# Two drains in GpSimd's order: a gated linear recurrence with routed experts on one Trainium2 core

## The chip, the cores and the metric

The kernel runs on one core of a Trainium2 chip. The time is that of one execution on the device, in microseconds (us). The engines are TensorE (PE in the profile, with its weight loads as PEld), VectorE (DVE), ScalarE (ACT), GpSimd (POOL) and SyncE (SP). A `q` behind an engine's name, as in POOLq, means its sequencer: instructions such as waits, register moves and drains, which the profile does not count as busy time.

## The reference

A recurrence with complex gates runs over 768 steps for 4 batches of 8 heads of width 48. Its output, 3072 rows of 384, goes through a mixture of 8 experts in which every row is given to one expert:

```python
for t in range(S):
    new_re = ar * S_re - ai * S_im
    new_im = ar * S_im + ai * S_re
    kv = np.einsum('bhd,bhe->bhde', k[:, :, t], v[:, :, t])
    S_re, S_im = (new_re + kv, new_im)
    y[:, :, t] = np.einsum('bhd,bhde->bhe', q[:, :, t], S_re)
...
logits = x @ w_gate                        # x: (3072, 384), 8 experts
expert_idx = np.argmax(logits, axis=1)
...
for e in range(E):                         # the rows of expert e, in sorted order
    h = np.maximum(x_sorted[lo:hi] @ w1[e], 0.0)
    y_sorted[lo:hi] = h @ w2[e]
y = y_sorted[inv_perm]
return (gate_w[:, None] * y).astype(np.float32)
```

## The kernel before

The first half, to about 280 us, computes the recurrence in six chunks of 128 steps and writes the rows `x` to a scratch array `xd` in device memory. While it does so, the router counts which rows go to which expert. The experts are then sorted by the number of their rows into eight **places**. Place 0 is the expert with the most rows; `CAPS = (448, 416, 416, 408, 400, 384, 376, 360)` gives the rows that each place has room for. A place is cut into tiles of 128 rows: four for places 0 to 4, three for places 5 to 7.

The second half is a loop over the places (`for i in range(E)`, L894). For place i:

- `gather` (L574, the instruction at L580) issues one indirect transfer for each tile on GpSimd, which fetches the rows from `xd` into `xg`. The gathers of the next place are written ahead of the expert's work.
- `turn` (L589) transposes the gathered rows on TensorE. The turn of the next place stands between the second-last and the third-last output tile of the present one.
- `expert` (L620) multiplies by the first weights into four buffers `hps`, evicts them with the ReLU on VectorE (L635) and ScalarE (L633) in turn, multiplies by the second weights into `yps`, and scales by the gate into `y` on VectorE (L655, or L666 to L669 for a tile of few rows). `y` comes from a pool `yp` of three buffers.
- `scatter` (L610, the instruction at L611) issues one indirect transfer for each tile on GpSimd, which writes the rows of `y` to their places in the output.
- `load_w` (L563) loads the weights of the place after next, on SyncE's queue.

The two tiles that place 0 does early (`early`, L672) run at the end of the first half. The last output tile of the last place is finished behind a branch: `verdict` (L877) tests whether the input lies in the range that the fast path covers, the branch at L909 leads to a slow path that these inputs do not take, and L1161 and L1162 then scale and scatter the last tile.

A planner of the framework sets the order of the instructions on each engine, from data dependences, priorities in the order of writing, and planned times. So gathers stand further ahead on GpSimd than they are written: those of place 6 are issued while place 3 is finished. `behind` (L70) adds an edge for order alone between two instructions:

```python
def behind(ins, others, reason="order"):
    for o in others:
        tc.add_manual_dep(ins.ins, o.ins.name, NOSYNC, reason=reason)
```

Besides the gathers and scatters, GpSimd issues four small transfers in the first half (L255). At the end of the program the framework puts closing code on every engine (L1186 in the profile): SyncE waits for all semaphores, GpSimd has a drain, and barriers join the engines.

Of the kernel before, what the change touches and what calls it, by code (L numbers as in the profile page):

```python
# [36 lines left out]
def kernel(  # L37
# [12 lines left out]
    nc = tc.nc  # L50
# [13 lines left out]
    T = {}  # L64

    def mm(o, lhsT, rhs, start=True, stop=True):
        T["mm"] = nc.tensor.matmul(o, lhsT=lhsT, rhs=rhs, start=start, stop=stop, skip_group_check=True)  # L67
        return T["mm"]
# [4 lines that stand above are left out]
# [487 lines left out]
    def tiles(i):  # L560
        return -(-CAPS[i] // P)

    def load_w(i, after=None):  # L563
        o = own0 if i == 0 else owner[:, i : i + 1]
        ev = nc.sync.value_load(o[0:1, 0:1], min_val=0, max_val=E - 1)
        wa = EP[i % 2].tile([P, KD, F], FP, tag="wa", name="wa")
        ins = nc.sync.dma_start(out=wa, in_=w1[ds(ev, 1)].rearrange("o (i p) f -> p (o i) f", p=P))
        if after is not None:
            tc.add_manual_dep(ins.ins, after.ins.name, SYNC, reason="rows first")
        wb = EP[i % 2].tile([P, KF, DM], FP, tag="wb", name="wb")  # L570
        nc.sync.dma_start(out=wb, in_=w2[ds(ev, 1)].rearrange("o (i p) d -> p (o i) d", p=P))
        T["w", i] = wa, wb

    def gather(i, t0, t1, rows=N):  # L574

        if t0 == 0:
            T["xg", i] = EP[i % 2].tile([P, CT, DM], FP, tag="xg", name="xg")
        for t in range(t0, t1):
            n = min(P, CAPS[i] - t * P)
            nc.gpsimd.indirect_dma_start(  # L580
                out=T["xg", i][0:n, t],
                out_offset=None,
                in_=xd[0:rows, :],
                in_offset=bass.IndirectOffsetOnAxis(ap=tok[0:n, i, t : t + 1], axis=0),
                bounds_check=rows - 1,
                oob_is_err=False,
            )

    def turn(i, t0, t1, ps, end=None):  # L589

        xg = T["xg", i]
        if t0 == 0:
            T["xt", i] = EP[i % 2].tile([P, KD, CAPS[0]], FP, tag="xt", name="xt")
        c0, c1 = t0 * P, min(CAPS[i], t1 * P)
        for d in range(KD):
            tp = ps.tile([P, 512], FP, tag="tp", name="tp")
            for t in range(t0, t1):
                n = min(P, CAPS[i] - t * P)
                ins = nc.tensor.transpose(
                    out=tp[:, (t - t0) * P : (t - t0) * P + n],  # L600
                    in_=xg[0:n, t, d * P : (d + 1) * P],
                    identity=ident[0:n, 0:n],
                )
                if end is not None:
                    behind(ins, [end])
            T["turned"] = (nc.scalar.copy if d % 2 else nc.vector.tensor_copy)(
                out=T["xt", i][:, d, c0:c1], in_=tp[:, 0 : c1 - c0]
            )

    def scatter(y, n, i, t, to=None):  # L610
        nc.gpsimd.indirect_dma_start(  # L611
            out=out,
            out_offset=bass.IndirectOffsetOnAxis(ap=row[0:n, i, t : t + 1] if to is None else to[0:n], axis=0),
            in_=y[0:n],
            in_offset=None,
            bounds_check=N - 1,
            oob_is_err=False,
        )

    def expert(i, t0, t1, psH, psO, yp, between=None):  # L620

        xt = T["xt", i]
        wa, wb = T["w", i]
        if t0 == 0:
            T["ht", i] = EP[i % 2].tile([P, KF, CAPS[0]], FP, tag="ht", name="ht")
        ht = T["ht", i]
        c0, c1 = t0 * P, min(CAPS[i], t1 * P)
        for f in range(KF):
            ps = psH.tile([P, 512], FP, tag="tp" if psH is psT else "h", name="hps")[:, 0 : c1 - c0]
            for d in range(KD):  # L630
                mm(ps, wa[:, d, f * P : (f + 1) * P], xt[:, d, c0:c1], d == 0, d == KD - 1)
            if f % 2:
                nc.scalar.activation(out=ht[:, f, c0:c1], in_=ps, func=AF.Relu)  # L633
            else:
                ts(out=ht[:, f, c0:c1], in0=ps, scalar1=0.0, scalar2=None, op0=OP.max)  # L635
        for t in range(t0, t1):
            if t == t1 - 2 and between is not None:
                between()
            n = min(P, CAPS[i] - t * P)
            if psO is psA:  # L640
                ps = psO.tile([P, DM], FP, tag="at", padded_shape=[P, 512], name="yps")
            else:
                T["left"] = T.get("left", sum(tiles(j) for j in range(E)) - EARLY) - 1
                po = psO if T["left"] % 2 else EP["last"]
                ps = po.tile([P, DM], FP, tag="y", padded_shape=[P, 512], name="yps")
            g = gate[0:n, i, t : t + 1]
            y = yp.tile([P, DM], FP, tag="y", name="y")
            hs = ht[:, :, t * P : t * P + n]
            if n > 64:
                for f in range(KF):  # L650
                    mm(ps[0:n], hs[:, f], wb[:, f], f == 0, f == KF - 1)
                if i == E - 1 and t == t1 - 1:
                    T["last"] = ps[0:n], g
                    return
                ts(out=y[0:n], in0=ps[0:n], scalar1=g, scalar2=None, op0=OP.mult)  # L655
            else:

                w = 32 if n <= 32 else 64
                parts = P // w
                for f in range(KF):  # L660
                    j = f % parts
                    mm(ps[j * w : j * w + n], hs[:, f], wb[:, f], f < parts, f >= KF - parts)
                z = yp.tile([P, DM], FP, tag="z", name="z")
                for j in range(1, parts):
                    nc.scalar.copy(out=z[j * w : j * w + n], in_=ps[j * w : j * w + n])
                tt(out=y[0:n], in0=ps[0:n], in1=z[w : w + n], op=OP.add)  # L666
                for j in range(2, parts):
                    tt(out=y[0:n], in0=y[0:n], in1=z[j * w : j * w + n], op=OP.add)
                ts(out=y[0:n], in0=y[0:n], scalar1=g, scalar2=None, op0=OP.mult)  # L669
            scatter(y, n, i, t)  # L670

    def early(t0, t1, end):  # L672
# [204 lines left out]
    def verdict():  # L877

        bad = yp.tile([P, NC + 1], FP, tag="bad", name="bad")
        nc.vector.memset(bad, 0.0)  # L880
        ts(out=bad[:, 0:NC], in0=inr, scalar1=float(RW) - 0.5, scalar2=None, op0=OP.is_lt)
        nc.vector.tensor_copy(out=bad[:, NC:], in_=over)
        bp = psG.tile([P, NC + 1], FP, tag="tp", padded_shape=[P, 512], name="bp")
        mm(bp, ones, bad)
        bs = yp.tile([P, 2], FP, tag="bs", name="bs")
        nc.vector.reduce_sum(bs[:, 0:1], bp[:, 0:NC], axis=AX_X)
        nc.vector.reduce_sum(bs[:, 1:2], bp, axis=AX_X)
        nc.vector.tensor_copy(out=flag, in_=bs[0:1])
        ts(out=bs[:, 1:2], in0=bs[:, 1:2], scalar1=0.0, scalar2=float(2 * N), op0=OP.is_gt, op1=OP.mult)
        tt(out=lasts, in0=row[:, E - 1, tiles(E - 1) - 1 : tiles(E - 1)], in1=bs[:, 1:2], op=OP.add)  # L890

    turn(0, EARLY, tiles(0), psG)
    load_w(1, T["turned"])
    for i in range(E):  # L894
        t0 = EARLY if i == 0 else 0
        if i == E - 1:
            verdict()
        if i + 1 < E:
            gather(i + 1, 0, tiles(i + 1))
        expert(i, t0, tiles(i), psH, psO, yp, (lambda: turn(i + 1, 0, tiles(i + 1), psG)) if i + 1 < E else None)  # L900
        if i + 2 < E:
            load_w(i + 2)
        if 1 <= i <= NR_:
            in_range(i - 1)
# [255 lines left out]
    y = ctx.enter_context(tc.tile_pool(name="lasty", bufs=1)).tile([P, DM], FP, name="y")  # L1160
    ts(out=y[0:n], in0=ps, scalar1=g, scalar2=None, op0=OP.mult)  # L1161
    scatter(y, n, E - 1, tiles(E - 1) - 1, lasts)  # L1162


# [26 lines left out]
```

## Time and profile before

| | |
|---|---|
| median of 3 runs | 562.87 us |
| the runs | 561.13 to 563.52 us |
| profiled execution, its own time | 566.46 us |
| span of the profile, first to last instruction | 564.7 us |
| TensorE busy | 533.7 us, 95% |
| GpSimd busy | 68.6 us, 12% |
| last scatter issued | 557.70 us from the span's start |

The span is what the profile covers; the profiled execution's own time is 1.8 us longer. Times within the profile count from the start of the span. A transfer's instruction on GpSimd is busy only while its descriptors are made; the data lands later.

### The profile page before, as it was taken

The page shows a single profiled execution, that of the slowest core. Times are in us where ns is not written, and L with a number is a line of the kernel's source. Part 1 is how long each engine was busy: PE and PEld are TensorE (multiplying, and loading weights), DVE is VectorE, ACT ScalarE, POOL GpSimd, SP SyncE. Part 2 cuts the span into 40 slices and gives each one's busy share as a digit, 9 for nine tenths or more (in the row PEclk, how much of TensorE's full clock was granted, in tenths as well). Part 3 has the DMA queues.
Part 4 walks back from the last instruction along what each step waited for, and adds up shares of the span by engine and source line. Part 5 has one row for each costly group of instructions (what it writes and reads, how often), then busy time and mean ns, then how long its engine had stood idle before and what let it go on. Part 6 is the DMA issues. An engine that isn't in the chain of part 4 may idle for free. (4 is left out here: it accounts for less than half of the span.)

```text
span 564.7 us, 8239 instructions
## 1 busy us (share of the span) xinstructions
PE 533.7 (95%) x3221; PEld 379.9 (67%) x3221; DVE 287.0 (51%) x586; ACT 218.2 (39%) x330; POOL 68.6 (12%) x94
## 2 busy tenths in 40 slices
PE   3889989999999999999899999999999999999994
PEld 2666858877888888888767555555565555565652
DVE  5478688678789889786366264412212131111200
ACT  6867887966678864553200010101101011010000
POOL 2000000000000000001044301503022030100101
PEclk9979979999999999999999999999999999999997
DMA  9976791859655835603549985533235333330000
GB/s 167 187 96 87 126 129 26 160 82 169 114 86 101 151 61 120 98 29 120 190 182 328 387 314 233 183 119 91 102 140 167 113 111 96 127 124 15 26 15 27
DMA packets 166053, 73.39 MB, mean 130 GB/s; under 512 B 147725, under 2 KB 159031, under 8 KB 166008
## 3 DMA queue, kind: packets, MB, share of 16 engines
q1 hardware_dynamic: 162456, 63.12, 48.1%
q0 software_dynamic: 3552, 9.68, 5.0%
q8 instruction: 27, 0.44, 0.4%
q14 instruction: 18, 0.15, 0.1%
HBM read 63.26 MB, written 9.73 MB: 129 GB/s over the span
## 5 line engine op out<-in xcount | busy, mean ns | idle before, releaser
L67 PE MATMUL yps<-wb,ht 128*128 128x384 f32 (+6 forms) x464 | 136.8, 489 | 0.0
L67 PE MATMUL hps<-xt,wa 128*128 128x416 f32 (+7 forms) x432 | 132.5, 465 | 0.0
L67 PEld LDWEIGHTS hps<-xt,wa 128*128 128x128 f32 x432 | 79.9, 190 | 49.8 <-issue 24.1
L67 PEld LDWEIGHTS yps<-wb,ht 128*128 128x128 f32 (+6 forms) x464 | 74.1, 175 | 52.9 <-issue 8.1
L633 ACT ACTIVATE ht<-hps 128x416 f32<-128x416 f32 (+7 forms) x36 | 16.8, 468 | 139.8 <-PE hps L67 128.5
L655 DVE TENSOR_SCALAR y<-yps,gate 128x384 f32<-128x384 f32 (+1 forms) x23 | 14.2, 617 | 99.4 <-PE yps L67 99.3
L67 PE MATMUL at<-qt,kt 96*128 96x128 f32 x384 | 54.2, 281 | 0.5 <-DVE am L334 0.5
L611 POOL DMA_INDIRECT out_dram<-y,row x28 | 28.7, 1023 | 191.4 <-DVE y L655 162.8
L67 PEld LDWEIGHTS at<-qt,kt 96*128 96x128 f32 x384 | 47.6, 191 | 4.8 <-issue 1.9
L635 DVE TENSOR_SCALAR ht<-hps 128x416 f32<-128x416 f32 (+7 forms) x36 | 18.9, 525 | 61.4 <-PE hps L67 61.4
L334 DVE TENSOR_TENSOR am<-at,tri 128x512 f32<-128x512 f32 x48 | 33.0, 688 | 21.0 <-PE at L67 20.9
L67 PE MATMUL yt<-am,v 128*48 128x128 f32 x384 | 43.0, 281 | 0.6 <-DVE am L334 0.6
L580 POOL DMA_INDIRECT xg<-xd,tok x29 | 31.6, 1089 | 78.6 <-PE tp L326 40.4
L67 PE MATMUL yt<-qt,G 96*48 96x128 f32 x320 | 36.7, 274 | 0.0
L326 PE MATMUL tp<-ident,K 128*96 128x128 f32 x192 | 33.7, 288 | 0.7 <-DVE K L317 0.4
L67 PE MATMUL dk<-v,K 128*96 128x48 f32 x320 | 33.7, 248 | 0.2 <-DVE G L365 0.2
L67 PEld LDWEIGHTS dk<-v,K 128*96 128x96 f32 x320 | 33.0, 171 | 1.3 <-issue 0.5
L326 PE MATMUL tp<-ident,Q 128*96 128x128 f32 x192 | 33.3, 281 | 0.1
L328 ACT COPY kt<-tp 96x512 f32<-96x512 f32 x48 | 28.0, 582 | 13.1 <-PE tp L326 12.9
L67 PEld LDWEIGHTS yt<-am,v 128*48 128x48 f32 x384 | 24.8, 122 | 8.2 <-DVE am L334 2.2
L328 ACT COPY qt<-tp 96x512 f32<-96x512 f32 x48 | 28.1, 586 | 3.6 <-PE tp L326 3.6
L255 POOL DMA_DIRECT2D ai<-cd x4 | 3.4, 841 | 215.1 <-ACT R L169 103.9
(159 smaller groups left out, 670.2 us busy)
## 6 DMA issues: line engine op xcount, KB each, us to landing
wa<-in_moe_w_dram SPq DMA_DIRECT2D x8, 1536.0 KB
wb<-in_moe_w_dram SPq DMA_DIRECT2D x8, 1536.0 KB
q<-in_q_dram SPq DMA_DIRECT2D x12, 384.0 KB
k<-in_k_dram SPq DMA_DIRECT2D x12, 384.0 KB
v<-in_v_dram SPq DMA_DIRECT2D x12, 384.0 KB
xd<-x SPq DMA_DIRECT2D x24, 192.0 KB
rc<-in_a_re_dram SPq DMA_DIRECT2D x6, 768.0 KB
rc<-in_a_im_dram SPq DMA_DIRECT2D x6, 768.0 KB
```

The source lines that it names most:

```text
L67: T["mm"] = nc.tensor.matmul(o, lhsT=lhsT, rhs=rhs, start=start, stop=stop, skip_group_check=True)
L255: nc.gpsimd.dma_start(out=T["ai", u][0:1, b0:b1].rearrange("p b h d -> p (b h d)"), in_=cd[1, u - 1 : u, b0 * DM : b1 * DM], accum_op=OP.add,)
L326: nc.tensor.transpose(out=tp[0:DD, j], in_=X[:, hg * 4 + j], identity=ident)
L328: nc.scalar.copy(out=t[0:DD], in_=tp[0:DD])
L334: tt(out=am, in0=at, in1=bc(tri, 1, 4), op=OP.mult)
L580: nc.gpsimd.indirect_dma_start(out=T["xg", i][0:n, t], out_offset=None, in_=xd[0:rows, :], in_offset=bass.IndirectOffsetOnAxis(ap=tok[0:n, ...
L611: nc.gpsimd.indirect_dma_start(out=out, out_offset=bass.IndirectOffsetOnAxis(ap=row[0:n, i, t : t + 1] if to is None else to[0:n], axis=0) ...
L633: nc.scalar.activation(out=ht[:, f, c0:c1], in_=ps, func=AF.Relu)
L635: ts(out=ht[:, f, c0:c1], in0=ps, scalar1=0.0, scalar2=None, op0=OP.max)
L655: ts(out=y[0:n], in0=ps[0:n], scalar1=g, scalar2=None, op0=OP.mult)
```

## The change

`scatter` keeps the instruction that it issued in `T["scattered"]`. A new function `drain` puts a drain instruction on GpSimd, ordered behind the last scatter issued, and keeps it in `T["drained"]`; each scatter from then on is ordered behind it. The loop over the places calls `drain` after the expert's work of places 3 and 6, which are the fourth and the seventh. The edges are for order alone, with no semaphore. Nothing else is changed.

```diff
     def scatter(y, n, i, t, to=None):
-        nc.gpsimd.indirect_dma_start(
+        ins = nc.gpsimd.indirect_dma_start(
             out=out,
...
             bounds_check=N - 1,
             oob_is_err=False,
         )
+        if "drained" in T:
+            behind(ins, [T["drained"]])
+        T["scattered"] = ins
+
+    def drain():
+
+        ins = nc.gpsimd.drain()
+        behind(ins, [T["scattered"]])
+        T["drained"] = ins
...
+    DRAINS = (3, 6)
     turn(0, EARLY, tiles(0), psG)
     load_w(1, T["turned"])
     for i in range(E):
...
         expert(i, t0, tiles(i), psH, psO, yp, (lambda: turn(i + 1, 0, tiles(i + 1), psG)) if i + 1 < E else None)
+        if i in DRAINS:
+            drain()
         if i + 2 < E:
             load_w(i + 2)
```

## The prediction

> **What bounds the kernel now.** I read the first two parts of the page, then the view of the tail by line, then GpSimd's order in time.
>
> ```profile
> PE 533.7 (95%) x3221; PEld 379.9 (67%) x3221; DVE 287.0 (51%) x586; ACT 218.2 (39%) x330; POOL 68.6 (12%) x94
> ...
> PE   3889989999999999999899999999999999999994
> ...
> POOL 2000000000000000001044301503022030100101
> ```
>
> Columns: busy microseconds, share of the span and instructions; then busy tenths in 40 slices of 14.1 us. TensorE fills every slice but the first and the last. GpSimd has 12%, so the drains are put on an engine that mostly waits. A gain must come from where TensorE is not the limit, and only the last slice is left: TensorE's last matmul ends before 557, the span at 564.7. The view of the tail's line, cut to its last 7 us, and SyncE's waits say what lies there.
>
> ```profile
> L1186 SPq EVENT_SEMAPHORE  x10: 17/28/28, 560.6 to 564.0; - x10
> L1186 SPq DRAIN  x2: 7/10/13, 561.1 to 561.2; - x2
> L1186 POOLq EVENT_SEMAPHORE  x2: 17/17/17, 563.9 to 564.0; - x2
> ...
> L1186 POOLq DRAIN  x1: 6427/6427/6427, 557.4 to 557.4; - x1
> ```
>
> ```profile
> SPq L1186 <- DMA out_dram<-y,lasts: 5.2, 1, 5.2
> ```
>
> Columns: shortest/median/longest in ns, first and last start in us; the line by itself is a wait of SyncE: its total, count and longest. The closing code already holds one GpSimd drain of 6.43 us. To two decimals it runs from 557.45 to 563.87. SyncE waits until 560.58 for the last scatter to land, goes through its list of semaphores, and its own drain ends at 561.20. All other engines are done earlier. GpSimd takes its next step at 563.92, and everything to the end of the span (0.8 us of barriers) follows that. So **the end is set by GpSimd's drain, 563.87 - 561.20 = 2.67 us later than SyncE would set it**.
>
> What the drain does in that time is not shown, but it can be sized. The last scatter's descriptors are made from 557.70 to 558.73 inside it, which leaves 5.14 us. Page rows give the transfers that GpSimd has issued by then: 4 (L255), 29 gathers (L580), 28 + 1 scatters (L611), **62 in all**, with no GpSimd drain among them. Other drains on the same engine, with no new transfer ahead of them, take 182 ns (L1177), 118 and 46 ns (L1186). A drain that takes 30 to 100 times as long behind 62 transfers, and goes on 3.3 us after the last has landed (560.56 in the semaphore records), looks like one that goes through the transfers one by one: 5.14 us / 62 = 83 ns each if it starts behind the descriptors, 3.31 / 62 = 53 ns if it starts at the last landing. Both are estimates from this one row.
>
> **What the Trainium skill says.** "PSUM — Partial Sum Buffer", Engine vs sequencer instructions: a "drain waits for the engine to go fully idle". The trace agrees: the last one outlasts the last scatter. "Perfetto Trace Analysis", DMA Instruction — SWDGE (GPSIMD): the bar of a GpSimd transfer ends when its descriptors are made, not when the data has moved. Here the bar of the scatter at 432.97 is 0.94 us and the landing 2.3 us after its start. "DMA: Bandwidth & Descriptors", Anatomy of one DMA: about 2.0 us of a small transfer are fixed; the landings here, 2.3 to 4.6 us, fit. No page prices a GpSimd drain behind many transfers.
>
> **The change, part by part.** It adds two GpSimd instructions. It removes nothing and moves nothing on SyncE's queue. The ordering edges carry no semaphore, since both ends are on GpSimd. GpSimd's order around the two places:
>
> ```profile
> 424.72 1.06 POOL L580 DMA_INDIRECT xg<-xd,tok  x1 [0.31 <-issue]
> 427.43 1.04 POOL L611 DMA_INDIRECT out_dram<-y,row  x1 [1.65 <-DVE y L655]
> 432.97 0.94 POOL L611 DMA_INDIRECT out_dram<-y,row  x1 [4.50 <-DVE y L669]
> 450.33 1.01 POOL L611 DMA_INDIRECT out_dram<-y,row  x1 [16.42 <-DVE y L655]
> ...
> 527.34 1.03 POOL L611 DMA_INDIRECT out_dram<-y,row  x1 [4.21 <-DVE bs L887]
> 547.21 1.00 POOL L611 DMA_INDIRECT out_dram<-y,row  x1 [18.84 <-DVE y L655]
> 552.37 0.99 POOL L611 DMA_INDIRECT out_dram<-y,row  x1 [4.16 <-DVE y L655]
> 557.70 1.03 POOL L611 DMA_INDIRECT out_dram<-y,lasts  x1 [4.35 <-DVE y L1161]
> ```
>
> Columns: start, length, what, and in brackets the idle time before it and who ended it.
>
> **First drain**, behind the scatter at 432.97 (the last of the fourth place). Its descriptors are done at 433.91; 46 of the 62 transfers are issued by then (4, 26 gathers, 16 scatters). At 83 ns each: 433.91 + 3.82 = 437.7. At 53 ns each behind the landing at 435.3: 435.3 + 2.4 = 437.7. Queued behind it is the first scatter of the fifth place, whose data is there at 450.3, then the gathers of the eighth at 456.77, used near 515. The idle time ahead of that scatter is 16.42 us: 12.6 us are left. Cost: nothing. Lower bound nothing, and if it took the closing drain's full 6.43 us, still nothing.
>
> **Second drain**, behind 527.34. If the first has struck its 46 off, 13 are left: 1.1 us by the first price, or the landing at 530.55 plus 0.7 us, so done by 531.3. Next on the engine is 547.21, 15.9 us later. Cost: nothing.
>
> **Closing drain.** Three transfers are left. At 83 ns they are gone through before the last landing; at 53 ns behind it, the drain ends at 560.56 + 0.16 = 560.7. Either is ahead of SyncE's 561.20. What is late next is thus SyncE, and the gain is 2.67 us. The remainder of the closing drain would have to exceed 0.64 us past the landing before it costs any of this. A further small term: the last scatter (104 rows) took 2.86 us to land beside the drain, while three of 128 rows at 515.86, 522.15 and 547.21 took 2.59 to 2.61 with GpSimd idle. If the drain's work slows it, that comes back, 0.27 us. If not, nothing. I take two thirds, 0.18.
>
> Sum: 2.67 + 0.18 = **2.85 us**. The profiled execution took 566.46 us (span 564.70 and 1.76 around it), which would become 563.6. It lies 3.6 us above the median of the three runs; the tail is a fixed piece that does not scale with that, so I take it off the median: 562.87 - 2.85 = **560.0 us**.
>
> **The rivals.**
>
> *A, as above.* For it: 62 transfers and a drain far longer than empty ones. Against it: only one GpSimd drain with transfers ahead of it is in the trace, so that its length grows with their number is not shown. Gain 2.67 to 2.94 us; with the spread of the runs (561.13 to 563.52) its own range is 558.9 to 561.2.
>
> *B, no gain.* The closing drain's length is not a matter of the number: a fixed settling of about 3.3 us behind the last landing, or a walk over all that was ever issued. Or the added drain does not wait for transfers at all. Then the two are hidden as worked out (435.3 + 3.3 = 438.6, still 11.7 us early) and the end stays: 562.9. For it: the 3.3 us past the landing. Against it: the drains of 118 and 46 ns right behind, for which nothing was new; a walk over everything would show there too.
>
> *C, slower.* The first drain holds GpSimd far longer than the gap. The place: output tiles y have three buffers, so the fourth y of the fifth place (DVE, 463.85) reuses that of the scatter at 450.33, which needs 2.6 us to land. The delay decides from the point at which GpSimd is free later than 461.2, a drain of over 27 us. Behind that DVE instruction stand the evictions of TensorE's four hps buffers, which are full at about 470. A drain of 40 us would free GpSimd at 473.9, y at 476.5, the first eviction a microsecond later: TensorE loses 7.4 us, the tail gains 2.7, 567.6 in all. Against it: 27 us are four times the closing drain, which had more transfers ahead of it. Even if the drain waited for every queue, no transfer packet is in flight from 434.8 to 445.2.
>
> **How the numbers follow.** A has 0.80, B 0.11, C 0.09. About 0.5% (2.8 us) is what a measurement of this kernel can tell from no change, and A's gain lies right at it. In A the losses are shut out by the 0.48 us between 560.7 and 561.20, so more lies above the mark than below it: 0.60 faster and 0.20 same. B gives 0.02, 0.07 and 0.02 with the spread of the runs. Faster 0.62, same 0.27, slower 0.11. The range takes A's own and reaches B on the upper side: 558.8 to 563.1, leaving out C and the ends.
>
> **What would show it.** Two new GpSimd drains, from about 434 to 438 and from about 528.4 to 531, with nothing moved behind them (the scatters still some 16 and 19 us apart). If the price is per transfer, the first goes on some 2.4 us behind its landing and the second well under 1. The closing drain down from 6.43 to about 3.2 us, ending before SyncE's. The time from the last scatter's start to the end of the span down from 7.0 to about 4.3 us. It is wrong if the closing drain still goes on some 3 us behind the landing (B), or if TensorE shows a new wait at 460 to 480 (C).

## The result and the profile after

The change makes the kernel faster by about half a percent: the ratio to the runs of before is 0.9951, 95% interval 0.9934 to 0.9969. On 562.2 us, the median of before beside those runs, that is 2.75 us. The median with the change is 559.33 us.

The page of the changed kernel, in the same three lines as before (busy time and shares, then slices of 13.9 us):

```profile
PE 529.4 (95%) x3221; PEld 376.8 (68%) x3221; DVE 286.6 (51%) x586; ACT 217.8 (39%) x330; POOL 68.4 (12%) x94
...
PE   3889979999999999999999999999999999999996
...
POOL 2000000000000000001054301403013040100101
```

The span fell from 564.7 to 556.9 us, far more than the runs did. Most of that is not the change's work: the scatter ahead of the first drain already starts 4.99 us earlier (427.98 against 432.97), when no drain has run. In the profile of before TensorE ran at half clock for two stretches of 6.8 us near 30 and 78 us, here for one of 3.4 us near 77 us. That is 10.2 us less at half clock, or some 5.1 us of full-speed work (an estimate from these stretches). What the change does is read from the **tail**: from the last scatter's start to the end of the span. It begins behind the last matmul, so TensorE's clock does not set it.

The closing code after the change (line L1198 now, from 552 to 556.2 us; name, count, shortest/median/longest in ns, first and last start in us), with SyncE's wait below it:

```profile
L1198 SPq EVENT_SEMAPHORE  x10: 17/28/28, 555.4 to 556.2; - x10
L1198 SPq DRAIN  x2: 7/10/13, 556.0 to 556.0; - x2
L1198 POOLq EVENT_SEMAPHORE  x2: 17/17/17, 556.1 to 556.1; - x2
...
L1198 POOLq DRAIN  x1: 3291/3291/3291, 552.3 to 552.3; - x1
```

```profile
SPq L1198 <- DMA out_dram<-y,lasts: 5.0, 1, 5.0
```

GpSimd's drain is 3.29 us where it was 6.43. To two decimals it ends at 555.56, and SyncE's own drain ends at 556.03: **the order of the two has turned round**, and GpSimd's next step (556.06) follows SyncE at once. The tail is 4.34 us against 7.03: 2.69 us less.

The two new drains (L625) and GpSimd's order around them:

```profile
L625 POOLq DRAIN  x2: 4122/4575/5028, 427.7 to 521.9; - x2
```

```profile
419.55 1.07 POOL L580 DMA_INDIRECT xg<-xd,tok  x1 [0.31 <-issue]
422.25 1.04 POOL L611 DMA_INDIRECT out_dram<-y,row  x1 [1.64 <-DVE y L664]
427.98 0.94 POOL L611 DMA_INDIRECT out_dram<-y,row  x1 [4.69 <-DMA out_dram<-y,row]
445.15 1.01 POOL L611 DMA_INDIRECT out_dram<-y,row  x1 [16.23 <-DVE y L664]
```

Start, length, what, and in brackets the idle time before it with who ended it. The first drain is 5.03 us from 427.73 to 432.76; the timeline does not list it, since drains are no busy time. The scatter behind it still waits 16.23 us, and for its data on VectorE, as before (16.42). The second is 4.12 us from 521.90 to 526.02, and the next scatter is at 542.03.

A drain's bar starts before the last transfer's descriptors are made (427.73 against 427.98 to 428.92 for the first). Two distances say more than its length: from the end of those descriptors to the end of the drain, and from the last landing to the end of the drain.

| drain | transfers since the last | past the descriptors, us | past the landing, us |
|---|---|---|---|
| before, closing | 62 | 5.14 | 3.31 |
| after, first | 46 | 3.84 | 2.49 |
| after, second | 13 | 2.82 | 0.57 |
| after, closing | 3 | 2.00 | 0.17 |

With many transfers the third column is 83 ns for each (5.14 / 62 and 3.84 / 46). With few, the landing sets the end and little follows. The landing itself did not move: 2.87 us from the last scatter's start, 2.86 before.

### The profile page after: what moved, and what is told of

The parts are those of the page before. It is cut to its first block, busy times and chain, and to the rows that moved or that the text cites. A ratio compares the mean times of both kernels' runs of the same rounds, so it can differ in the third digit from the quotient of the medians.

```text
span 556.9 us, 8241 instructions
## 1 busy us (share of the span) xinstructions
PE 529.4 (95%) x3221; PEld 376.8 (68%) x3221; DVE 286.6 (51%) x586; ACT 217.8 (39%) x330; POOL 68.4 (12%) x94
## 4 chain that ended last, share of the span: by engine, by line
PE 80%; issue 6%; DVE 5%; DMA 4%; ACT 4%; POOLq 0%; POOL 0%; ACTq 0%
PE yps L67 22%; PE hps L67 22%; PE tp L326 7%; PE at L67 7%; PE yt L67 7%; PE dk L67 4%; PE cst L67 4%; PE xb L67 3%; PE csl L67 3%; PE tp L599 2%; DMA xg<-xd,tok 1%; DMA xd<-x 1%; PE sp L67 1%; ACT R L169 1%; DMA carry<-cd 1%
```

## The experiments

The theory: the closing drain pays for each transfer that GpSimd has issued and that no earlier drain has already paid for, and an earlier drain takes that payment to a place where GpSimd has nothing to do. The rivals: the second drain needs the first, or only a late one helps; the ordering edges or the planner's order gained it; the price is for rows or is a fixed settling; drains cost something of their own.

The times do not tell one, two, seven and 28 drains apart: their ratios lie between 0.9934 and 0.9964, with intervals that overlap. So each run is read from its tail too.

**One drain instead of two.** First the one of the seventh place alone:

```diff
-    DRAINS = (3, 6)
+    DRAINS = (6,)
```

> One drain alone, behind the last scatter of the seventh place. It has 59 transfers ahead of it. Theory (a price for each transfer, behind the last landing): the drain goes on 59 x 53 ns = 3.1 us past the landing of its scatter and is over some 13 us before the next scatter; the closing drain has three transfers left, takes about 3.3 us and ends before SyncE's; gain as with both drains, ratio about 0.995. Rival (the first drain is needed too, for instance since the second would run into the work of the last place): the closing drain or the last scatters come later than with both, and the gain is smaller by over 0.5 us.

Measured: ratio 0.9947 (0.9928 to 0.9967). The drain, with 59 transfers, ends 4.90 us past its descriptors (83 ns each) and 2.55 past its landing, at 528.8, 13.9 us ahead of the next scatter. The tail is 4.33 us. One drain does the work of both, as long as its gap is wide enough for all of it; of the expectation only the 3.1 us past the landing were too many.

Then the one of the fourth place alone, `DRAINS = (3,)`:

> One drain alone, behind the last scatter of the fourth place. 46 transfers are ahead of it, 16 are left to the closing drain. At 53 ns each behind the last landing the closing drain goes on 0.85 us past the landing, 0.2 us past SyncE's end: the tail (last scatter's start to the end of the span) is 4.5 to 4.6 us against 4.36 with both. At 83 ns each behind the descriptors of the last scatter it would have gone through all 16 before the landing, and ends within 0.2 us of it: tail 4.36. Rival (only a drain shortly ahead of the end helps): tail about 7.0 as before.

Measured: ratio 0.9934 (0.9909 to 0.9959), tail 4.43 us. The closing code, from 555 to 559.6 us:

```profile
L1198 SPq DRAIN  x2: 7/10/13, 559.4 to 559.4; - x2
...
L1198 POOLq DRAIN  x1: 3831/3831/3831, 555.7 to 555.7; - x1
L1198 POOLq EVENT_SEMAPHORE  x1: 17/17/17, 559.5 to 559.5; - x1
```

With 16 transfers left the drain ends at 559.49, 0.70 us behind the landing and 0.06 us behind SyncE's end (559.42): just the point at which it begins to show in the tail, by 0.09 us against both drains. Neither price by itself gives this: 53 ns each behind the landing is 0.85 us, and 83 ns from the descriptors on would have been over before it. Some 44 ns are paid behind the landing.

**Is it the drain, or the place in the order?** A memset of one column stands in the drain's place, with the same edges:

```diff
-        ins = nc.gpsimd.drain()
+        ins = nc.gpsimd.memset(spare, 0.0)
```

> A memset of one column of a spare tile on GpSimd in place of each of the two drains, with the same ordering edges. Theory: the closing drain still has 62 transfers ahead of it, 6.4 us, tail 7.0 us, ratio 1.000 (0.998 to 1.002). Rival (the order or the planner's times are what gained): closing drain or the tail shorter, ratio near 0.995.

Measured: ratio 0.9988 (0.9969 to 1.0008), no change within the interval; tail 7.03 us, that of before to the hundredth. Drains and memsets apart, the traces show the instructions of each engine, by operation and tile, in the same order before, after and here. The closing drain (L1199 in that kernel, the longest of its three):

```profile
L1199 POOLq DRAIN  x3: 46/118/6425, 555.1 to 562.1; - x3
```

An instruction and its edges at these places bring nothing. The drain does.

**More transfers.** The kernel before, with five small gathers written behind each of six places (the planner issues all 30 early, from 293 to 349 us):

```diff
+        if 1 <= i <= 6:
+            for x in range(5):
+                nc.gpsimd.indirect_dma_start(
+                    out=spare[0:16, x],
+                    out_offset=None,
+                    in_=xd[0:N, :],
+                    in_offset=bass.IndirectOffsetOnAxis(ap=tok[0:16, i, 0:1], axis=0),
...
         if i + 2 < E:
             load_w(i + 2)
```

> The kernel before with 30 further small gathers of 16 rows each into a spare tile that nobody reads, five behind each of the places 1 to 6; no drain but the closing one. 92 transfers instead of 62, 6,760 rows instead of 6,280. Theory (a price for each transfer): the closing drain goes on 92 x 53 ns = 4.9 us past the last landing, tail 8.6 us against 7.0. Rival (a price for each row or descriptor): 3.3 x 6760 / 6280 = 3.6 us past the landing, tail 7.3 us. Rival (a fixed settling): 3.3 us, tail 7.0.

Measured: the closing drain is 8.88 us, 7.59 past the descriptors (82.5 ns for each of 92), 5.76 past the landing; tail 9.48 us. The number of transfers counts, not that of rows: the 30 added 2.45 us to the drain, 82 ns each, though they carry an eighth of the rows that 30 full tiles would, and all of them were issued over 200 us ahead of it. The expected 4.9 us behind the landing was again the 53 ns price, which does not carry over to another number.

The ratio, 1.0095 (1.0057 to 1.0132), is 5.4 us on the 563.75 us of before beside it (3.2 to 7.4 by the interval), more than the tail's 2.45. Part of the rest is in the small gathers' own place: they stand ahead of a scatter on GpSimd, so it lands late, and a scaled tile waits for its buffer:

```profile
350.62 1.04 POOL L611 DMA_INDIRECT out_dram<-y,row  x1 [0.31 <-issue]
...
353.36 0.62 DVE L655 TENSOR_SCALAR y<-yps,gate 128x384 f32<-128x384 f32 x1 [3.79 <-DMA out_dram<-y,row]
...
354.03 1.50 PE L67 MATMUL yps<-wb,ht 128*32 128x384 f32 x16 [1.76 <-DVE y L655]
```

TensorE (last line) stands still for 1.76 us behind VectorE, which waits for a scatter's landing. The slower rival needed this path, though it had the wait pass on through the `hps` buffers, and here it passes through `yps`. The path exists, but two drains in wide gaps don't open it.

**A drain behind each of the first seven places,** `DRAINS = (0, 1, 2, 3, 4, 5, 6)`:

> A drain behind the last scatter of each of the first seven places, with 24, 8, 7, 7, 7, 3 and 3 transfers new to each. Theory (a price for each transfer not yet struck off, about 82 ns from the last descriptors on where there are many, landing plus about 44 ns each where there are few): lengths past the descriptors of 24 x 82 = 2.0 us or landing plus 1.1 us for the first, landing plus 0.3 us for those of seven or eight, landing plus 0.15 us for those of three; all hidden in gaps of 13 to 19 us; tail 4.35 us, ratio as with two, 0.995. Rival (each drain costs TensorE something of its own): slower than with two by over 0.3%.

Measured: ratio 0.9942 (0.9921 to 0.9962), tail 4.35 us. Past their landings the seven drains go on 1.04 us (24 transfers), 0.37 (8), 0.32 three times (7) and 0.16 twice (3). A straight line through these is 0.03 us and 42 ns for each transfer. The first runs for 6.89 us, most of it waiting for the landing in a busy stretch of the transfers; it is hidden too.

**A drain too late.** No drain in the gaps, and one behind the second scatter of the last place:

```diff
             scatter(y, n, i, t)
+            if i == E - 1 and t == t1 - 2:
+                drain()
```

> One drain alone, behind the last but one scatter that the loop issues (the second of the eighth place), 5.3 us ahead of the last scatter. 61 transfers are ahead of it. Theory: 61 x 82 ns = 5.0 us past the descriptors, that is to about the time at which the last scatter was due, with the branch and its register work still to come on GpSimd's sequencer: the last scatter starts 1 to 2.7 us late behind its data, the closing drain has one transfer and ends before SyncE's. From the last matmul's end to the end of the span 6.5 to 8.1 us, against 8.1 before and 5.45 with the change: most of the gain is gone, ratio 0.997 to 1.000. Rival (the walk runs beside the sequencer's work and the next transfer, and costs nothing anywhere): 5.45 us, ratio 0.995.

Measured: ratio 1.0014 (0.9993 to 1.0035), worse than the range expected. GpSimd in time, with VectorE's last scaling between its two scatters, then the drain, the branch's last step on GpSimd and the semaphore waits ahead of that scaling:

```profile
550.99 0.98 POOL L611 DMA_INDIRECT out_dram<-y,row  x1 [4.15 <-DVE y L664]
...
558.93 0.62 DVE L1175 TENSOR_SCALAR y<-yps,gate 104x384 f32<-104x384 f32 x1 [8.22 <-DMA out_dram<-y,row]
560.01 1.03 POOL L611 DMA_INDIRECT out_dram<-y,lasts  x1 [8.04 <-DVE y L1175]
```

```profile
L625 POOLq DRAIN  x1: 6278/6278/6278, 550.8 to 550.8; - x1
```

```profile
L923 POOLq INC_SWDGE_SEM  x1: 188/188/188, 558.4 to 558.4; - x1
```

```profile
L1175 DVEq EVENT_SEMAPHORE  x6: 50/50/4331, 554.1 to 558.8; - x6
```

The same waits in the kernel before:

```profile
L1161 DVEq EVENT_SEMAPHORE  x6: 49/50/965, 555.3 to 555.8; - x6
```

The drain ends at 557.03, 5.06 us past its descriptors (61 transfers, 83 ns each), and only then does GpSimd's sequencer read the flag of the branch (557.08) and go on, to the end of `INC_SWDGE_SEM` at 558.60. VectorE is held by that: the 4331 ns are a wait from 554.26 to 558.59, for a semaphore that rises at 558.56, within this instruction. Before, its longest wait there (965 ns) was the one for the last matmul. So the last scaling starts 3.71 us behind the last matmul's end (555.22; 0.19 before), and the last scatter 4.79 us behind it, against 1.11 before. The closing drain, with one transfer, ends well ahead of SyncE, and from the last matmul's end to the end of the span are 9.13 us (8.14 before, 5.45 with the change). The payment was moved onto the path, with the branch's own work and VectorE's scaling behind it. The scatter did wait for `y`, as its bracket says; the scaling's bracket names a transfer, but the last one ahead of it had landed at 553.69.

**A drain with nothing left to land.** In place of the change's two drains stand two that are held back, each by a copy on GpSimd that reads a block of the next place, until the transfers have long landed:

```diff
+        if i - 1 in (3, 6):
+            cpy = nc.gpsimd.tensor_copy(out=spare, in_=ht[:, 4, 0:48])
+            behind(cpy, [T["scattered"]])
+            drain()
+            behind(T["drained"], [cpy])
         for t in range(t0, t1):
```

> The two drains as in the change, but each behind a small copy on GpSimd that reads the fifth evicted block of the next place, so that it starts some 5 us after its scatter, when all transfers have landed for 3 us. 46 and 13 transfers. Theory of one price for every transfer wherever the landing is, 82 ns: 3.8 and 1.1 us from the end of the copy. Theory of a price behind the landing alone, 53 ns: 2.4 and 0.7 us. Theory of waiting for landings (no work of its own): under 0.2 us each. Tail 4.35 us in all three, ratio 0.995.

```profile
L626 POOLq DRAIN  x2: 1367/2734/4100, 434.5 to 532.0; - x2
```

The two copies inside these bars take 0.22 us each. From their ends the drains take 3.85 us for 46 transfers and 1.12 us for 13: 84 and 86 ns each, starting 3.6 and 6.2 us after everything has landed. So a drain pays for each transfer even if nothing is outstanding. Tail 4.38 us, ratio 0.9959 (0.9938 to 0.9979).

**A drain behind each of the 28 scatters of the loop and of the early tiles:**

> A drain behind every scatter of the loop and of the early tiles, 28 in all. Theory: the first has some 13 transfers, the others one to six each; each holds GpSimd to the landing of its scatter plus 0.05 to 0.3 us, about 2 us past the descriptors. Tail 4.2 to 4.4 us. In places 0 and 1 the gathers of the next place stand behind them and come up to 3 us later; if TensorE has no reserve there, it waits 0 to 6 us and the ratio is 0.995 to 1.005; if it has, 0.995 as with two drains.

Measured: ratio 0.9964 (0.9938 to 0.9989), tail 4.33 us. The bars are 2.3 to 12.7 us, the longest around places 0 and 1, where transfers are dense and land late. They end 1.2 to 6.8 us past their descriptors, where about 2 were expected. A drain with one transfer ends 0.07 to 0.08 us past its landing. TensorE is busy for 45.15 of the 46 us from 280 to 326, where the gathers stand behind these drains (44.91 with two drains), and for all of the 89 us after that: it has reserve there. One drain does cost: the last of the 28 (547.51 to 550.40) stands ahead of the branch and delays it, as in the run with the late drain. From the last matmul's end to the end of the span are 5.71 us, against 5.45 with two drains.

## Why the prediction was right

- **The bound.** The end was set by GpSimd's closing drain, 2.67 us behind SyncE. It now ends 0.47 us ahead of SyncE (0.48 forecast, with the end 0.16 us past the landing; measured 0.17). The tail lost 2.69 us.
- **The number.** 2.85 us were forecast, 2.75 measured (1.7 to 3.7 by the interval). The interval is far wider than the 0.10 us between them, so that closeness is luck; the tail's 2.69 us beside the 2.67 of the main term is what bears the forecast out.
- **The mechanism.** Of rival B (a fixed settling, a walk over all that was ever issued, or an added drain that does not wait for transfers) nothing is left: 3, 13, 16, 46, 59, 62 and 92 transfers give lengths that follow the number since the last drain, and the memset shows that the order alone gains nothing.
- **The cover.** The first drain ends 3.84 us past its descriptors (3.82 forecast) and leaves 12.4 us (12.6); the second 0.57 us past its landing (at most 0.7). SyncE was rightly named as what is late next.
- **What was mis-sized.** The term of 0.18 us for a quicker last landing is nothing: the landing takes 2.87 us with a short closing drain, 2.86 with a long one. Why it takes longer than the 2.6 us of the others stays open. The closing drain of before is 35 to 140 times as long as the empty ones (6427 ns against 182 to 46), not 30 to 100. And the two prices were both made from one row, where they had to agree. 83 ns from the descriptors on holds for 46 to 92 transfers; 53 ns behind the landing does not (63 ns each at 92, 44 at 16). What fits all the rows is two terms: about 41 ns each from the end of the descriptors on, then the wait for the landing if it is not over, then about 42 ns each. For 62: 558.73 + 2.54 = 561.27, which is past the landing at 560.56; + 2.60 = 563.87, as measured. That a drain goes through its list twice is a reading of the lengths, and no run here shows it from inside.
- **The slower rival (C).** Its sign did not come: from 415 to 527 us TensorE is busy for all of the 112 us, before and after. Its place, the y buffers, is real, and the small gathers opened it. Its trigger, a drain of over 27 us, is far off: the longest of all the drains tried is 12.7 us. The way to lose the gain is another one: a drain with too little time ahead of the next thing that GpSimd has to do, as the late one shows.

## What to carry to other kernels

Where GpSimd issues many transfers, look at how long its closing drain goes on past the last landing, and whether another engine's end is later anyway. If it sets the end, one drain in a gap of GpSimd, late enough to leave few transfers behind it and early enough for 83 ns times the transfers before it, takes the difference off; more drains, or drains beyond the point where another engine ends last, gain nothing. Don't put it where GpSimd is due soon: a drain holds back the register and branch work behind it too, and with that any engine that waits for this work.

## What the runs showed of the hardware

A GpSimd drain was expected to wait. It also takes time for each transfer since the last drain: 82 to 86 ns where the landing does not cover a part of it, even when all landed microseconds before, and 82 ns for transfers of 16 rows too. The instruction `INC_SWDGE_SEM` that the framework puts behind the branch on GpSimd grows with the same number, more cheaply: 0.19 us with no transfer since the last drain (0.03 at the start of the program), 0.24 with 2, 0.50 with 15, 1.42 with 61 and 2.03 with 91, which is 20 ns each on top of the 0.19. It does not stand in for a drain: behind it the closing drain of before still took 83 ns for each of 62. VectorE's last scaling waits for it, as the late drain shows. In the kernel before it ended at 554.89, 1.7 us ahead of the last matmul's end (556.60), so its fall from 1.42 to 0.24 us brought nothing here.
